# Attention and two feed-forward layers on one core: float32 scores for eight head pairs, read-backs as scheduled loads, and another sequence of value products

## The chip, the core and the metric

The kernel runs on one NeuronCore of a Trainium2 chip. TensorE multiplies matrices, VectorE (DVE), ScalarE (ACT) and GpSimd (POOL) work elementwise, and SyncE (SP) issues the DMAs. Each engine takes its instructions strictly in the order in which the program lists them, so an instruction that waits holds back all that stand behind it on the same engine. The metric is device microseconds of the whole launch, the median of several runs.

## The reference

```
q_n, k_n = rmsnorm(q, g_q), rmsnorm(k, g_k)          # 4 batches x 12 heads, 448 rows of 64
scores = q_n @ k_n.T / 8
attn = exp(scores - max(scores)); attn /= attn.sum() + 1e-9
x = (attn @ v) -> 1792 tokens x 768
x = relu(x @ w_in)**2 @ w_out                        # layer 1, 2048 wide
out = (silu(x @ w_gate) * (x @ w_val)) @ w_out2      # layer 2, 1536 wide
```

Everything is float32. A product of two float32 matrices is mostly made of three faster products: each operand is split into a high part that the fast float32r format holds exactly and a low remainder, and high x high, high x low and low x high are added up (`mm3`).

## The kernel before

Heads are taken in 24 pairs (7 tiles of 128 rows by 448 columns each, since 2 x 448 = 7 x 128; tile 3 holds rows of both heads). For each tile TensorE makes the scores (`sc`, L723 and L729), DVE takes the row maximum (L751) and scales it (L754), ACT takes the exponential into `ring` (L760), TensorE transposes (`pt`, L818 to L828), ACT or DVE copies the result out (`p`, L218), and TensorE multiplies by the values (`o`, L881); DVE divides by the row sums (`ox`, L895).

Scores come in two forms. A pair listed in `FULL_S` is multiplied in float32 straight from the loaded tile `kq_p`: one instruction of the program for a tile, which the trace shows as two (L723). For any other pair `prep_k` and `prep_q` first split k and q of each head into high and low parts (`kst`, `qst`: casts on ACT, subtractions on POOL or DVE, L639 to L660), and TensorE makes two float32r products for each head in a tile, 16 for a pair (L729). Before, `FULL_S` holds pair 0 alone.

While pairs are worked, TensorE fills gaps with products of layer 1 for two finished batches (`h_a`, `ya`: "filler"), and DVE decodes weights, which come as 64-bit words. A first few dozen transposes of the identity (`warm`, L1002) run at the very start.

After attention, layer 1 runs in seven sweeps over a batch (x tokens of 448) and a range of the hidden width. Each needs its activations read back from DRAM and split (`xr` and `x`, `load_x`), and sweeps that finish an earlier partial sum read it back too (`yp`, `Partial`), add to it (L1190) and store it. The raw tiles come from a pool of seven, `io`. Layer 2 takes batches in two pairs and forms each 2x2 block product with seven products instead of eight (`PRODUCTS`, a Strassen-like scheme): operands of weights are formed ahead and spilled to DRAM (`md`), then read into `ring` as `mr` and split; operands of activations are `xq` and `xm` (`x_quarter`, `x_rest`). For each of six steps `fp` there is a gate stage (`hp_g`), a value stage (`hp_v`) and an output stage (`yo`), which wants `s_v` of the value stage, the second half of the hidden rows first (b = 1: products 3 and 7).

The order of everything is made by a planner inside the program. Work items are generator threads with a rank; each yields costs in ns per engine that may do it, a bare number (wait so long), or a condition. `simulate` steps a clock and hands each free engine the ready item of lowest rank. What it emits is a fixed order for each engine; semaphores do the waiting on the chip. A DMA issued through `dma(...)` costs the planner time and continues the thread when the planner thinks it has landed. In `Partial.load` before, the read of a partial sum is issued directly and is known to the planner as no work at all: the tile counts as there at once. In `load_x` before, one tile is read, cast and subtracted before the next is asked for.

## Time and profile before

| | us |
|---|---|
| median of 3 runs | 1338.75 (1335.79 to 1339.97) |
| the profiled execution | 1345.3 |
| its span, first to last instruction | 1343.5 |
| TensorE busy | 1273.7 (95%) |
| DVE busy | 1029.4 (77%) |
| ACT busy | 674.3 (50%) |
| POOL busy | 221.3 (16%) |

In the rows below, "busy" is the time in which at least one instruction of an engine runs; PEclk is the granted share of TensorE's clock, 1.00 for 2.4 GHz and 0.50 for 1.2 GHz. In a row of the timeline, x6 means six like instructions in a row, and the bracket gives the engine's idle time before the first and what ended it. Consecutive matmuls overlap, so their rate is read from start to start.

### The profile page before, as it was taken

How to read it: one execution, taken by the hardware profiler on the slowest of the kernel's cores; microseconds unless marked ns; L12 is line 12 of the kernel's file. 1: busy time of each engine (PE TensorE's matmuls, PEld its weight loads, DVE VectorE, ACT ScalarE, POOL GpSimd, SP SyncE). 2: the span in 40 equal slices, each digit the busy share in tenths (PEclk: the TensorE clock that was granted, in tenths of full speed). 3: DMA queues.
4: the chain of work that ended last, by engine and by line, in shares of the span. 5: the costliest groups of instructions: out<-in, count | busy, mean ns of one | idle time of the engine just before them, and what ended most of it. 6: DMA issues, size and time to landing. Idle time of an engine off the chain costs nothing.

```text
span 1343.5 us, 19657 instructions
## 1 busy us (share of the span) xinstructions
PE 1273.7 (95%) x6306; PEld 1077.3 (80%) x6306; DVE 1029.4 (77%) x2262; ACT 674.3 (50%) x1528; POOL 221.3 (16%) x207
## 2 busy tenths in 40 slices
PE   8787899998999999999999998899999999999998
PEld 6544576666777999999998897799989889999997
DVE  7999997865641788978877897989885687666573
ACT  5788897876854455443332333543443355333331
POOL 3444444543331000000000101010110130000000
PEclk8789999999999999999999899899999989999999
DMA  5676666676422355468687795475443452322222
GB/s 199 202 227 209 199 214 196 204 220 182 154 78 72 104 157 163 139 204 255 198 264 237 234 327 183 148 224 161 148 127 89 141 169 85 106 83 83 82 65 82
DMA packets 125129, 222.13 MB, mean 165 GB/s; under 512 B 17177, under 2 KB 98658, under 8 KB 125026
## 3 DMA queue, kind: packets, MB, share of 16 engines
q1 hardware_dynamic: 125026, 220.89, 52.5%
q8 instruction: 49, 0.80, 0.2%
q14 instruction: 54, 0.44, 0.1%
HBM read 176.03 MB, written 44.80 MB: 164 GB/s over the span
## 4 chain that ended last, share of the span: by engine, by line
PE 69%; DVE 16%; DMA 7%; issue 3%; ACT 2%; SPq 1%; POOL 1%; DVEq 0%; ACTq 0%; POOLq 0%
PE y L341 19%; PE h L341 12%; PE hp_v L341 10%; PE hp_g L341 7%; PE yo L341 6%; PE sc L729 3%; PE o L881 3%; PE h_a L341 2%; DMA zb<-zd 2%; PE ya L341 2%; DVE mr L1339 2%; DVE sc L751 2%; PE pt L828 2%; DVE f_g L1446 1%; DMA rkb<-rkd 1%
## 5 line engine op out<-in xcount | busy, mean ns | idle before, releaser
L341 PE MATMUL y<-s,hi_out 128*128 128x448 f32 x624 | 180.1, 370 | 3.1 <-DVE yp L1190 3.1
L341 PE MATMUL h<-x,hi_in 128*128 128x448 f32 x588 | 167.8, 366 | 1.6 <-DVE r L378 1.6
L751 DVE TENSOR_REDUCE sc<-sc 128x1 f32<-128x448 f32 x168 | 101.8, 625 | 51.8 <-PE sc L729 47.8
L760 ACT ACTIVATE ring<-sc,m,rms 128x448 f32<-128x448 f32 x168 | 121.8, 726 | 34.8 <-DVE m L754 25.0
L341 PEld LDWEIGHTS y<-s,hi_out 128*128 128x128 f32 x624 | 118.6, 190 | 13.6 <-ACT wa_g L272 3.4
L729 PE MATMUL sc<-kst,qst 128*128 128x448 f32 x368 | 110.6, 407 | 15.3 <-ACT ring L760 12.4
L218 ACT CAST mr<-mr 128x384 fp32r<-128x384 f32 x216 | 103.7, 512 | 39.1 <-DMA mr<-md_v_s 10.8
L341 PEld LDWEIGHTS h<-x,hi_in 128*128 128x128 f32 x588 | 110.3, 188 | 11.3 <-DVE r L378 2.0
L1339 DVE TENSOR_TENSOR mr<-mr 128x384 fp32r<-128x384 f32 x194 | 107.9, 577 | 14.8 <-ACT mr L218 14.8
L341 PE MATMUL y<-s,lo_out 128*128 128x448 f32 x312 | 115.0, 369 | 0.0
L341 PE MATMUL hp_g<-xm_t,mr 128*128 128x448 f32 x432 | 98.4, 377 | 10.5 <-DVE xm_t L1364 4.6
L341 PE MATMUL h<-x,lo_in 128*128 128x448 f32 x294 | 107.3, 365 | 0.0
L1446 DVE TENSOR_TENSOR f_v<-f_v,hp_v 128x448 f32<-128x448 f32 x60 | 37.0, 617 | 87.1 <-PE hp_v L341 87.1
L341 PE MATMUL yo<-s_v,mr 128*128 128x448 f32 x432 | 96.1, 378 | 6.2 <-ACT s_v L218 3.8
L218 ACT COPY p<-pt 128x448 f32<-128x448 f32 x166 | 86.2, 530 | 27.6 <-PE pt L828 20.7
L341 PEld LDWEIGHTS hp_g<-xm_t,mr 128*128 128x128 f32 x432 | 82.6, 193 | 20.1 <-DVE xm_t L1364 5.0
L341 PEld LDWEIGHTS yo<-s_v,mr 128*128 128x128 f32 x432 | 82.1, 193 | 18.9 <-DVE f_g L1446 4.7
L341 PE MATMUL hp_v<-xm_t,mr 128*128 128x448 f32 x432 | 94.0, 366 | 0.0
L341 PE MATMUL y<-s_v,mr 128*128 128x448 f32 x432 | 89.9, 366 | 0.0
L729 PEld LDWEIGHTS sc<-kst,qst 128*128 128x128 f32 x368 | 64.4, 199 | 29.2 <-ACT ring L760 16.0
L341 PEld LDWEIGHTS hp_v<-xm_t,mr 128*128 128x128 f32 x432 | 81.2, 188 | 6.8
L341 PEld LDWEIGHTS y<-s_v,mr 128*128 128x128 f32 x432 | 81.1, 188 | 6.8
(174 smaller groups left out, 2621.8 us busy)
## 6 DMA issues: line engine op xcount, KB each, us to landing
kq<-in_kq_t_dram SPq DMA_DIRECT2D x46, 448.0 KB
raw_in<-in_w_in_dram SPq DMA_DIRECT2D x32, 384.0 KB
raw_out<-in_w_out_dram SPq DMA_DIRECT2D x32, 384.0 KB
vz<-in_v_z_dram SPq DMA_DIRECT2D x23, 448.0 KB
rkb<-rkd SPq DMA_DIRECT2D x46, 224.0 KB
raw_o<-in_w_out_dram SPq DMA_DIRECT2D x24, 384.0 KB
raw_g<-in_w_gate_dram SPq DMA_DIRECT2D x24, 384.0 KB
raw_v<-in_w_val_dram SPq DMA_DIRECT2D x24, 384.0 KB
```

Source lines behind the costliest of these rows:

```text
L218: e.copy(out, src)
L341: return {"P": 203}, lambda e: e.matmul(ps, lhsT=w, rhs=x, start=first, stop=last), 0
L729: e.matmul(sc, lhsT=qs[h][:, c, rows], rhs=ks[h], start=(p + c == 0), stop=(p + 1 == len(parts) and c == 1),)
L751: yield {"V": 531}, lambda e: e.tensor_reduce(out=top, in_=sc, axis=AX.X, op=ALU.max, negate=True)
L760: yield {"A": 704}, lambda e: e.activation(out=probs(n, 0, S), in_=sc, func=ACTF.Exp, bias=m, scale=rq, accum_out=sums[g][0][:, i:i + 1])
L828: e.transpose(ps[:, bass.ts(t, 128)], probs((first if j < 3 else second) + t, k, 128), ident)
L881: e.matmul(o[half], lhsT=vz[:, j, half], rhs=ps[j][0], start=(i < 2), stop=(i >= 6))
L1339: yield {"W": 469, "G": 956}, lambda e: e.tensor_tensor(out=lo, in0=as_f32(lo), in1=as_f32(hi), op=ALU.subtract)
L1446: return {"V": 535}, lambda e: e.tensor_tensor(out=out, in0=b, in1=ps, op=how)
```

## The change

`FULL_S` grows from pair 0 to pairs 0 to 7: seven more pairs have their scores made in float32, without `prep_q` and the split of `prep_k`; DVE scales k once for a pair. `warm` goes on: until 90 us of the planner's clock it adds two transposes wherever the planner sees TensorE idle for over 300 ns. It holds a PSUM bank meanwhile that the filler needs. `load_x` starts a thread for each tile, so that several reads are under way, and leaves 3000 ns after the planned landing before it lists the cast. `Partial` reads its tiles through `dma(...)` in threads of their own, with 1500 ns after it. The product with operands (12, 21), which was third of seven, comes last in value stages, and the weights are read in that sequence. `RAW_SLOTS` goes from 7 to 8, which leaves 16 - 5 - 8 = 3 slots instead of 4 for `mr` at the start of layer 2; `x_fetch` leaves three `io` tiles instead of two to others.

```diff
-RAW_SLOTS = 7
+RAW_SLOTS = 8
+X_MARGIN = 3000
+IO_KEPT = 3
-WARM = [1500, 5500, 20000]
-FULL_S = [0]
+WARM = [1500, 5500, 20000, 90000]
+IDLE = 300
+FULL_S = list(range(8))
...
+        while clock[0] < WARM[3]:
+            yield 400
+            if clock[0] - free_at["P"] > IDLE:
+                for _ in range(2):
+                    yield {"P": 110}, lambda e: e.transpose(ps[:, :128], ident, ident), 0
         h_free.append(where)
...
-        def part(j, where):
+        def part(j, where, t):
             raw = tile_at(where, [128, S], F32, f"xr_{n}_{j}")
             yield from dma(lambda e: e.dma_start(out=raw, in_=src[j]), 128 * S * 4)
-            t = tiles(j)
+            yield X_MARGIN
             yield {"A": 467, "W": 300}, lambda e: copy(e, t[:, 0, :], raw)
...
         for j in range(KD):
             yield lambda: io_free
-            yield from part(j, io_free.pop(0))
+            spawn(part(j, io_free.pop(0), tiles(j)), k)
...
         def load(self):
-            while io_free and len(self.tiles) < KD:
-                j = len(self.tiles)
-                self.at[j] = io_free.pop(0)
-                self.tiles[j] = tile_at(self.at[j], [128, S], F32, f"yp_{self.n}_{j}")
-                nc.sync.dma_start(out=self.tiles[j], in_=self.src[j])
+            while io_free and self.next < KD:
+                spawn(self.one(self.next, io_free.pop(0)), self.k)
+                self.next += 1
+
+        def one(self, j, where):
+            t = tile_at(where, [128, S], F32, f"yp_{self.n}_{j}")
+            yield from dma(lambda e: e.dma_start(out=t, in_=self.src[j]), 128 * S * 4)
+            yield MAT_MARGIN
+            self.at[j], self.tiles[j] = where, t
...
+    ORDERS = {"g": PRODUCTS, "v": PRODUCTS[:2] + PRODUCTS[3:] + [PRODUCTS[2]]}
...
-            keys = [(w, fp, m) for _, m, _ in PRODUCTS]
...
+                keys = [(w, fp, m) for _, m, _ in ORDERS[w]]
...
-        keep = [0, 2] if p == 0 else [0, FLATS_KEPT]
+        keep = [0, IO_KEPT] if p == 0 else [0, FLATS_KEPT]
...
-        for i, m, x in PRODUCTS:
+        for i, m, x in ORDERS[w]:
```

On TensorE, the scores of pair 1 (`kst2`, `kst3` are the split k of its two heads, `kq_p1` its loaded tile) stand before as

```order
L729 MATMUL sc7_664<-kst2_636,qst0_247 128x448 x2
L729 MATMUL sc8_670<-kst2_636,qst0_247 128x448 x2
L729 MATMUL sc9_676<-kst2_636,qst0_247 128x448 x2
L729 MATMUL sc10_681<-kst2_636,qst0_247 128x448 x2
L729 MATMUL sc10_681<-kst3_639,qst1_248 128x448 x2
L729 MATMUL sc11_709<-kst3_639,qst1_248 128x448 x2
L729 MATMUL sc12_720<-kst3_639,qst1_248 128x448 x2
```

and now as

```order
L726 MATMUL sc7_621<-kq_p1_293 128x448
L726 MATMUL sc8_648<-kq_p1_293 128x448
L726 MATMUL sc9_656<-kq_p1_293 128x448
L726 MATMUL sc10_667<-kq_p1_293 128x448
L1010 MATMUL warm_264<-ident_205 128x128 x4
L726 MATMUL sc11_685<-kq_p1_293 128x448
L726 MATMUL sc12_693<-kq_p1_293 128x448
```

Sixteen float32r products of a pair become seven in float32, with four transposes of the identity among these. Up to the first score of pair 8, 31 products of the filler stand on TensorE before, and 15 now.

On DVE, where layer 1 ends and layer 2 begins (`yp_1_6` are the partial sums of the last sweep, `xm0` operands of the first batch pair, `f_0_g0_6` the first sum that frees a PSUM bank), there stands before

```order
L1190 TENSOR_TENSOR yp_1_6_2_9277<-y_1_6_2_8948,yp_1_6_2_9277 128x448
L1190 TENSOR_TENSOR yp_1_6_3_9286<-y_1_6_3_8958,yp_1_6_3_9286 128x448
L1364 TENSOR_TENSOR xm0_t2_1_9269<-xq0_12_1_8810,xm0_t2_1_9269 128x448
L1364 TENSOR_TENSOR xm0_t2_2_9270<-xq0_12_2_8933,xm0_t2_2_9270 128x448
L1383 TENSOR_TENSOR xq0_11_1_8809<-xq0_12_1_8810,xq0_11_1_8809 128x448
L1383 TENSOR_TENSOR xq0_11_2_8923<-xq0_12_2_8933,xq0_11_2_8923 128x448
L1383 TENSOR_TENSOR xq0_21_1_8914<-xq0_12_1_8810,xq0_21_1_8914 128x448
L1190 TENSOR_TENSOR yp_1_6_4_9327<-y_1_6_4_8966,yp_1_6_4_9327 128x448
L1446 TENSOR_TENSOR f_0_g0_6_9320<-f_0_g0_1_9299,hp_0_g0_6_9295 128x448
```

and now

```order
L1378 TENSOR_TENSOR xm0_t2_2_9045<-xq0_12_2_8729,xm0_t2_2_9045 128x448
L1378 TENSOR_TENSOR xm0_t3_1_9046<-xq0_11_1_8599,xm0_t3_1_9046 128x448
L1397 TENSOR_TENSOR xq0_11_2_8719<-xq0_12_2_8729,xq0_11_2_8719 128x448
L1378 TENSOR_TENSOR xm0_22_0_9047<-xq0_22_0_8597,xm0_22_0_9047 128x448
L1397 TENSOR_TENSOR xq0_21_2_8744<-xq0_12_2_8729,xq0_21_2_8744 128x448
L1378 TENSOR_TENSOR xm0_t3_2_9083<-xq0_11_2_8719,xm0_t3_2_9083 128x448
L1378 TENSOR_TENSOR xm0_22_1_9048<-xq0_22_1_8601,xm0_22_1_9048 128x448
L1378 TENSOR_TENSOR xm0_22_2_9094<-xq0_22_2_8737,xm0_22_2_9094 128x448
L1378 TENSOR_TENSOR xm0_t4_0_9049<-xq0_21_0_8598,xm0_t4_0_9049 128x448
L1202 TENSOR_TENSOR yp_1_6_3_9062<-y_1_6_3_8733,yp_1_6_3_9062 128x448
L1202 TENSOR_TENSOR yp_1_6_4_9069<-y_1_6_4_8741,yp_1_6_4_9069 128x448
L1460 TENSOR_TENSOR f_0_g0_6_9101<-f_0_g0_1_9076,hp_0_g0_6_9073 128x448
```

The operands of t2 no longer stand behind the additions of `yp` 3 that wait for a read; nine operations on operands come ahead of `yp` 3 and 4, and `f_0_g0_6` still stands behind both.

On TensorE, the end of the last value stage of the first batch pair and the start of its output stage, before:

```order
L341 MATMUL hp_0_v5_3_11525<-xm0_22_2_9378,mr102_11216 128x448 x3
L341 MATMUL hp_0_v5_4_11545<-xm0_t4_0_9271,mr103_11237 128x448 x3
L341 MATMUL hp_0_v5_4_11545<-xm0_t4_1_9333,mr103_11237 128x448 x3
L341 MATMUL hp_0_v5_4_11545<-xm0_t4_2_9379,mr103_11237 128x448 x3
L341 MATMUL yo0_5_0_11565<-s2_0_v5_3_11577,mr104_11254 128x448 x3
```

and now:

```order
L344 MATMUL hp_0_v5_4_11362<-xm0_t4_2_9095,mr102_11055 128x448 x3
L344 MATMUL hp_0_v5_2_11386<-xm0_21_0_8691,mr103_11075 128x448 x3
L344 MATMUL hp_0_v5_2_11386<-xm0_21_1_8967,mr103_11075 128x448 x3
L344 MATMUL hp_0_v5_2_11386<-xm0_21_2_8971,mr103_11075 128x448 x3
L344 MATMUL yo0_5_0_11401<-s2_0_v5_3_11409,mr104_11093 128x448 x3
```

Eighteen matmuls instead of nine now stand between product 3 and the first matmul that wants its result.

## Rows read from the trace of the kernel before

**Rows 1.** By stage: us, busy us of each engine, granted clock, DMA share

```profile
39.60:152.80 113.20, 89.04 (x441) 55.71 (x439) 107.07 (x265) 93.39 (x233) 47.89 (x41) 0.92 0.70 218
152.80:440.00 287.20, 273.63 (x1487) 200.17 (x1487) 187.83 (x479) 203.75 (x523) 111.44 (x98) 0.98 0.53 166
440.00:735.00 295.00, 295.00 (x1451) 271.88 (x1450) 250.50 (x558) 121.29 (x242) 3.12 (x3) 1.00 0.61 192
735.00:752.00 17.00, 12.32 (x46) 10.52 (x45) 16.46 (x34) 6.24 (x13) 3.40 (x3) 0.80 0.78 256
...
824.00:856.00 32.00, 21.30 (x79) 17.35 (x78) 21.23 (x41) 14.37 (x29) 5.25 (x5) 0.79 0.53 170
...
1071.00:1082.00 11.00, 7.00 (x21) 5.51 (x20) 9.09 (x14) 7.05 (x15) 5.43 (x5) 0.69 0.49 159
```

**Rows 2.** TensorE's timeline: float32 scores of pair 0, then split scores

```profile
15.20 1.70 PE L723 MATMUL sc<-kq_p 128*128 128x448 f32 x2
16.69 5.37 PE L1002 MATMUL warm<-ident 128*128 128x128 f32 x32
...
22.46 1.29 PE L723 MATMUL sc<-kq_p 64*128 64x448 f32 x3
...
23.59 0.91 PE L723 MATMUL sc<-kq_p 64*128 64x448 f32 x2
...
106.57 1.46 PE L729 MATMUL sc<-kst,qst 128*128 128x448 f32 x6
107.87 0.27 PE L826 MATMUL pt<-ident,ring 128*128 128x128 f32 x1
```

**Rows 3.** Groups from 39.6 to 152.8 us, DVE and POOL: count, busy, mean ns

```profile
L643 DVE TENSOR_TENSOR kq<-kq,rkb 128x448 f32<-128x448 f32 x9 | 6.6, 728 | 0.7 <-DMA rkb<-rkd 0.7
L640 DVE SCALAR_TENSOR_TENSOR kq<-kq,gqk,rkb 128x448 f32<-128x448 f32 x4 | 2.7, 679 | 0.0
...
L283 DVE SCALAR_TENSOR_TENSOR wt_in<-wa_in,wt_in 128x384 int32<-128x384 int32 x8 | 5.3, 667 | 0.0
...
L660 POOL TENSOR_TENSOR qst<-kq,qst 128x448 fp32r<-128x448 f32 x14 | 17.3, 1236 | 31.6 <-ACT qst L218 24.7 <-DMA vz<-in_v_z_dram 2.7 <-DVE rst L442 2.6
L648 POOL TENSOR_TENSOR kst<-kq,kst 64x448 fp32r<-64x448 f32 x12 | 15.1, 1259 | 17.3 <-ACT kst L218 12.3 <-ACT nat L465 4.5
```

**Rows 4.** DVE from 440 to 735 us, where POOL is idle: the same decoding step

```profile
L283 DVE SCALAR_TENSOR_TENSOR wt_in<-wa_in,wt_in 128x384 int32<-128x384 int32 x18 | 9.9, 551 | 0.0
```

**Rows 5.** The granted clock around the transposes of the identity, columns as in rows 1

```profile
13.30:20.20 6.90, 6.90 (x23) 4.65 (x22) 6.04 (x20) 1.79 (x4) 2.96 (x3) 0.51 0.41 111
20.20:30.40 10.20, 7.48 (x42) 4.72 (x40) 8.62 (x32) 8.35 (x23) 2.93 (x3) 1.00 0.44 134
...
78.20:85.00 6.80, 6.80 (x22) 3.18 (x22) 6.70 (x19) 6.20 (x18) 4.45 (x4) 0.50 0.88 281
```

**Rows 6.** Timeline around 735 us, SP, ACT and DVE

```profile
728.17 0.46 SPq L1100 DMA_DIRECT2D xr<-x1d  x1
...
734.70 0.57 ACT L218 CAST x<-xr 128x448 fp32r<-128x448 f32 x1 [10.55 <-DMA xr<-x1d]
...
735.30 0.63 DVE L1103 TENSOR_TENSOR x<-xr,x 128x448 fp32r<-128x448 f32 x1 [6.18 <-ACT x L218]
```

**Rows 7.** Timeline from 826 to 847 us, DVE and TensorE

```profile
830.87 0.62 DVE L1190 TENSOR_TENSOR yp<-y,yp 128x448 f32<-128x448 f32 x1 [2.51 <-DMA yp<-y1d]
837.37 0.62 DVE L1190 TENSOR_TENSOR yp<-y,yp 128x448 f32<-128x448 f32 x1 [3.20 <-DMA yp<-y1d]
...
832.08 1.87 PE L341 MATMUL hp_g<-xm_t,mr 128*128 128x448 f32 x5 [4.60 <-DVE xm_t L1364]
846.65 2.98 PE L341 MATMUL hp_g<-xm_t,mr 128*128 128x448 f32 x7 [3.04 <-DVE mr L1339]
```

**Rows 8.** TensorE at the end of the first batch pair

```profile
1069.64 2.02 PE L341 MATMUL hp_v<-xm_t,mr 128*128 128x448 f32 x9
1074.78 0.66 PE L341 MATMUL yo<-s_v,mr 128*128 128x448 f32 x1 [3.13 <-ACT s_v L218]
```

More of the change, by code (lines that the diff above doesn't have):

```diff
@@ L1094, in x_tiles, with load_x @@
         return tile_of
-    def load_x(src, n, tiles, done):
-        def part(j, where):
+    def load_x(src, n, tiles, done, k):
+        def part(j, where, t):
             raw = tile_at(where, [128, S], F32, f"xr_{n}_{j}")
             yield from dma(lambda e: e.dma_start(out=raw, in_=src[j]), 128 * S * 4)
-            t = tiles(j)
+            yield X_MARGIN
             yield {"A": 467, "W": 300}, lambda e: copy(e, t[:, 0, :], raw)
@@ L1134, in products @@
                     src = (x1_d if sweeps[i + 1][0] == 1 else x2_d)[sweeps[i + 1][1]]
-                    spawn(load_x(src, n, x_tiles(n, i % 2 == 0, nxt), done), k)
+                    spawn(load_x(src, n, x_tiles(n, i % 2 == 0, nxt), done, k), k)
                 if f == fs[1] and i + 1 == len(sweeps):
@@ L1151, in products @@
                     yield from behind.pop(0)
-                sums = Partial(partial, n) if partial and f == fs[-1] else None
+                sums = Partial(partial, n, k) if partial and f == fs[-1] else None
                 behind.append(out_of(name, n, layer, f, f == fs[0], f == fs[-1], f in last_use, ys, sums, dst, k))
@@ L1171, in attention_two_ffn_kernel, with __init__ @@
     class Partial:
-        def __init__(self, src, n):
-            self.src, self.n, self.tiles, self.at = src, n, {}, {}
+        def __init__(self, src, n, k):
+            self.src, self.n, self.k, self.next, self.tiles, self.at = src, n, k, 0, {}, {}
             self.load()
         def load(self):
-            while io_free and len(self.tiles) < KD:
-                j = len(self.tiles)
-                self.at[j] = io_free.pop(0)
-                self.tiles[j] = tile_at(self.at[j], [128, S], F32, f"yp_{self.n}_{j}")
-                nc.sync.dma_start(out=self.tiles[j], in_=self.src[j])
+            while io_free and self.next < KD:
[6 more added lines that the diff above has]
+            self.at[j], self.tiles[j] = where, t
     def written(ps, sums, j, n, dst):
@@ L1324, in ring_feed @@
         for k, (p, w, fp) in enumerate(stages()):
-            keys = [(w, fp, m) for _, m, _ in PRODUCTS]
             if w == "o2":
                 keys = [(w, 2 * fp + f, c) for f in range(2) for c in range(2)]
+            else:
+                keys = [(w, fp, m) for _, m, _ in ORDERS[w]]
             for key in keys:
```

## The prediction

> **What bounds the kernel now.** The page comes first: TensorE is busy for 95% of the span, DVE for 77%. An average over stages hides where time can be had, so the table by stage comes next [rows 1]. Three kinds of stretch are to be seen in it. From 39.6 to 152.8 us (the scores of pairs 1 to 7) TensorE is busy 89.0 of 113.2 us and DVE 107.1, so DVE is nearly full, TensorE idles 24.2 us, and the granted clock is 0.92. From 152.8 to 440 TensorE idles 13.6 of 287.2 us, and from 440 to 735 not at all: there only less TensorE work would help. Three short stretches stand out: 735 to 752 (12.3 of 17.0 busy, clock 0.80), 824 to 856 (21.3 of 32.0, 0.79) and 1071 to 1082 (7.0 of 11.0, 0.69). Together they hold 4.7 + 10.7 + 4.0 = 19.4 us of idle. Last come the timelines of these, where the bracket names the wait.
>
> **Float32 scores for pairs 1 to 7.** At full clock three instructions of a float32 score start at 22.46 and the fourth at 23.59, so 0.377 us each and 0.754 for a tile of two [rows 2]. Six split products start at 106.57 and the next row at 107.87, so 0.217 each [rows 2]. A pair is now 7 x 0.754 = 5.28 us instead of 16 x 0.217 = 3.47; over seven pairs TensorE gains 12.7 us of work. New transposes stand at 26 places of the order; at a sixth of a microsecond (5.37 us for 32, rows 2, at half clock) they are at most 4 us, and I take 2, since they stand where TensorE was meant to idle.
>
> What goes is preparation. On POOL the two subtractions are 17.3 + 15.1 = 32.4 of its 47.9 us [rows 1, 3]. On DVE the scalings of k are 6.6 + 2.7 = 9.3 us [rows 3]; seven float32 pairs put one back each, 7 x 0.68 = 4.8. DVE gains more than that, because its own work is slow while POOL runs: the same decoding step takes 667 ns here [rows 3] and 551 where POOL is idle [rows 4], 17% of its time. DVE work of this kind is about 60 of its 107 us (the rest are the reductions and what reads PSUM), so some 10 us are such waiting, and two thirds of POOL's time goes: 7 us. DVE comes to 107.1 - 9.3 + 4.8 - 7 = 96.
>
> TensorE's 89.0 us contain work at half clock: 0.92 granted is 18 of 113 us at 1.2 GHz, and at a busy share of 0.79 that cost 7. With 12.7 and 2 more, and 16 filler products fewer before pair 8 (31 before, 15 now, 16 x 0.21 = 3.3), TensorE has 100 us with that loss and 93 without. So DVE and TensorE both want about 95, and a chain through scores, maximum, exponential and transposes will not pack either fully. I take 102 for the stretch, a gain of 11; the 3.3 us of filler come back later, where TensorE is full [rows 1]. **Term: -8.** Bounds: no wait left at all, 95, is -18 + 3 = -15; nothing hidden, every idle microsecond and the low clock kept, is 12.7 + 2 = +15. The row nearest is DVE's 107 of 113, and it says that DVE was what the stretch waited for, so I stay on the side of a gain. From 152.8 to 440 the work is as before and I put 0.
>
> **The clock in idle spells.** From 16.69 to 21.98 nothing but transposes of the identity ran on TensorE [rows 2]; the granted clock was 0.51 up to 20.2 us and 1.00 after it [rows 5], so here transposes alone were followed by the rise to 2.4 GHz. Against this change speaks the Trainium skill (TensorE: Matmul & The Clock Gate, Part 4: PE-mode transpose): it says that full clock does not engage for transposes, since they do not count as busy in the same way. The trace does not bear that out. By the rule the new transposes would leave the low clock as it is, and TensorE would want 100 us in this stretch and not 93.
>
> **Activations read back, around 735 us.** The read of `xr` is issued at 728.17, and ACT, with the cast already at the head of its queue, stands idle 10.55 us until 734.70; DVE idles 6.18 us behind it [rows 6]. Behind these stand the squares of `h` that free a PSUM bank, so TensorE idles 4.7 us in the stretch, and clock 0.80 of 17 us is another 3.4 lost. After the change the planner lists the cast 3 us later than its planned landing, with other ACT work ahead of it. **Term: -7**, bounds 0 and -8.1; late next would be the additions of `yp`, which stand on DVE just behind.
>
> **Sums read back, 824 to 856.** The planner thought `yp` there at once, so DVE stands 2.51 and 3.20 us at additions whose reads are still on the way [rows 7], and behind them stand the operands of t2 (TensorE 4.60 us), sums that free banks, and the split of `mr` (3.04) [rows 7]. Idle is 10.7 us, and clock 0.79 of 32 costs 6.7 more: 17.4 in all. Now the operands come first, and with three `io` tiles instead of two the six sums need fewer rounds of store and read. But `mr` starts with three slots instead of four: the fourth weight is issued on SP behind two reads of sums, which wait for stores, then cast behind three casts of operands; and `f_0_g0_6` still stands behind two sums, with nine operations of 0.54 us or so ahead of them. I estimate 3 us of wait at the fourth product and 1 or 2 at the sixth, and part of the low clock. **Term: -9**, bounds -17 (all gone) and +3 (the new wait for `mr` beside the old ones).
>
> **Value products in another sequence.** At 1069.64 the last nine products of the value stage start, and `yo` starts at 1074.78 after 3.13 us of idle [rows 8]; a second wait makes it 4.0, and clock 0.69 of 11 us adds 3.4. Nine more products, 9 x 0.21 = 1.9 us, now stand between product 3 and its reader. On DVE the addition for product 2 stands ahead of the last step of `s_v` though, so about half of the idle stays. **Term: -3.5**, bounds 0 and -7.4. In other value stages a gate stage lies between, and the sequence costs nothing; u is held four products longer, and what hides that is that two of eleven flat tiles are still free.
>
> **The sum:** -8 - 7 - 9 - 3.5 = -27.5. The profiled execution took 1345.3, so it would be 1317.8; that execution was 6.5 above the median of the runs, and from 1338.75 the sum gives 1311.
>
> **Rivals.**
>
> *Slower: the float32 scores run at half clock.* The tile at 15.20 took 1.49 us to the next start at 16.69 [rows 2], at clock 0.51 [rows 5], twice the 0.754. If TensorE keeps its idle in this stretch and a share s of the 49 tiles runs so, the stretch is 15 + 36 s longer, against 19.5 gained later; from s = 0.15 on the kernel is slower, and at one half it is 15 + 18 - 19.5 = +13.5, 1352. For it: 18 of 113 us were at half clock before, and the filler, which padded such gaps, moves back. Against: each float32 tile keeps TensorE occupied for 0.75 us where there were 0.43, and at 78.2 to 85.0 the low clock met a TensorE without a gap [rows 5], so the low spells are rather what follows earlier idling, which shrinks.
>
> *The early stretch stays a chain of waits.* DVE is relieved but each pair still waits for exponential, transpose and copy; idle and clock stay, float32 is simply added: +15 - 19.5 = -4.5, 1334. For it: float32 scores leave the chain with as many steps as it had. Against: DVE at 107 of 113.
>
> *Transposes do not hold the clock.* The early term is -1 instead of -8: -20.5, 1318. The page named above says so; rows 5 speak against it.
>
> *Three slots for weights spoil the start of layer 2.* The third term is 0: -18.5, 1320. For it: the place of the fourth `mr` behind the sums. Against: the two DVE waits of rows 7 are for sums, and fewer rounds of these remain.
>
> **Chances.** Forecast 0.50, early chain 0.17, three slots 0.13, transposes 0.12, half-clock scores 0.08. A change of 0.3% (4 us) is about what a measurement of this kernel can tell from none. The forecast and the two rivals near 1320 are faster; of the early chain half is faster, the rest the same or a little slower; the half-clock case is slower. That makes 0.84, 0.06 and 0.10. The forecast's own range is 1300 to 1323. All best ends together, -15 - 8 - 17 - 7 = -47, give 1292, and the early chain with a little loss on top 1336; the range 1292 to 1336 leaves out the half-clock case and little else.
>
> **What would show it.** In the changed profile: pair 8's first score at about 142 us instead of 152.8 (the first term), with DVE no longer above 0.9 of the stretch; clock above 0.95 there, if the transposes help; no ACT idle of over 3 us for `xr`, and no TensorE idle near the fifth sweep's end; at the start of layer 2 under 6 us of idle, its first wait for `mr` and not for an operand; about 2 us before `yo` at the end of the first batch pair. The forecast is wrong in its main part if pair 8 starts no earlier than before, or if the idle of the three short stretches is still above 15 us.

## The result, and the profile after

The changed kernel takes 1326.48 us (median of 14 runs, 1320.24 to 1334.92); the kernel before took 1338.66 beside it (14 runs). The ratio is 0.9909, interval 0.9891 to 0.9926: 12.2 us faster. The forecast was 1311, that is 27.5 us faster; the sign was right, the size not, though the time lies in the range. The profiled execution took 1327.7 us (span 1325.9). The one before took 1345.3, which was 6.6 above its median, so the two profiles differ by 17.6 us and the medians by 12.2; below, it is said which of the two a number comes from.

Columns as in [rows 1], of the changed kernel: the same work, that is pairs 1 to 7, the stretch around the read of `xr`, the start of layer 2, the end of the first batch pair.

```profile
38.30:148.70 110.40, 105.17 (x431) 49.62 (x429) 95.33 (x273) 79.58 (x203) 19.31 (x19) 0.92 0.58 180
...
714.40:731.40 17.00, 17.00 (x85) 15.61 (x84) 15.25 (x33) 5.16 (x10) 0.00 (x0) 1.00 0.94 322
810.10:842.10 32.00, 27.27 (x123) 23.77 (x123) 31.42 (x57) 16.07 (x32) 8.71 (x7) 0.95 0.67 207
1050.50:1061.50 11.00, 6.00 (x21) 4.55 (x21) 10.82 (x15) 7.07 (x16) 7.05 (x6) 0.81 0.51 158
```

Against [rows 1]: TensorE's idle in the early stretch fell from 24.2 to 5.2 us and DVE's load from 107.1 to 95.3, but the stretch is only 2.8 us shorter, and the clock is 0.92 as before. The stretch at `xr` has no idle left. At the start of layer 2 TensorE is busy 27.3 of 32 us (21.3 before). The last row is no better than before: 6.0 of 11 us busy.

Two groups that answer to [rows 3, 4]: the split scores' scalings and subtractions are all but gone, and the decoding step takes 551 ns here too, where it took 667 beside POOL.

```profile
L286 DVE SCALAR_TENSOR_TENSOR wt_in<-wa_in,wt_in 128x384 int32<-128x384 int32 x8 | 4.4, 551 | 0.0
...
L643 DVE SCALAR_TENSOR_TENSOR kq<-kq,gqk,rkb 128x448 f32<-128x448 f32 x1 | 0.7, 673 | 0.0
```

ACT at the cast of `xr` (10.55 us of idle in [rows 6]) now idles a quarter of that, and nothing waits behind it:

```profile
722.45 0.57 ACT L221 CAST x<-xr 128x448 fp32r<-128x448 f32 x1 [2.54 <-DMA xr<-x1d]
```

DVE and TensorE at the start of layer 2, answering to [rows 7]: the additions of `yp` wait for no read, and the operands come first. The waits left are 3.20 us at the fourth gate product, for a sum `f_g` that stands on DVE behind operands and two `yp`, and 1.42 us before the first value product.

```profile
815.82 1.41 DVE L1378 TENSOR_TENSOR xm_t<-xq,xm_t 128x448 fp32r<-128x448 f32 x1
817.15 1.14 DVE L1202 TENSOR_TENSOR yp<-y,yp 128x448 f32<-128x448 f32 x2
818.22 0.60 DVE L1460 TENSOR_TENSOR f_g<-f_g,hp_g 128x448 f32<-128x448 f32 x1
...
818.97 5.23 PE L344 MATMUL hp_g<-xm_t,mr 128*128 128x448 f32 x18 [3.20 <-DVE f_g L1460]
829.34 2.06 PE L344 MATMUL hp_v<-xm,mr 128*128 128x448 f32 x9 [1.42 <-ACT sg_g L1510]
```

TensorE at the end of the first batch pair, answering to [rows 8]: the wait did not shrink, it came apart into 0.80, 1.12 and 3.08 us, the last for DVE.

```profile
1052.12 2.09 PE L344 MATMUL hp_v<-xm,mr 128*128 128x448 f32 x9 [0.80 <-DVE f_v L1460]
1055.33 0.48 PE L344 MATMUL yo<-s_v,mr 128*128 128x448 f32 x1 [1.12 <-ACT s_v L221]
1058.89 7.35 PE L344 MATMUL yo<-s_v,mr 128*128 128x448 f32 x23 [3.08 <-DVE s_v L1523]
```

By stretches of the same work, in the two profiles (start to start of the matmuls named, us):

| stretch | before | after |
|---|---|---|
| first scores of pairs 1 to 8 | 113.2 | 110.4 |
| first score of pair 8 to first score of the last pair | 230.1 | 219.4 |
| from there to the last products `o`, with the filler that is left | 37.1 | 45.2 |
| fifth to sixth sweep of layer 1 (`xr`) | 52.1 | 44.2 |
| first gate stage of layer 2 | 29.0 | 19.2 |
| first value product to first `yo` of the last step | 221.1 | 226.0 |

In these two profiles the read-backs won what was forecast (7.9 and 9.8 us), the early part won less, and the first batch pair, where 3.5 us were to be won, lost 4.9. The execution before was a slow one in two of these stretches. From pair 8 to the last pair, three experiments with its early order (e2, e3, e12) took 222.4 to 225.8 us and not 230.1. From the last `o` to layer 2, which the read of `xr` lies in, it took 404.7 us and six experiments with the old read-backs 399.8 to 403.3; with the new ones it is 396.8 to 397.0. So the usual gain there is 3 to 6.5 us and not 7.9.

### The profile page after: what moved, and what is told of

Its sections match the earlier page's. It is cut to its first block, busy times and chain, and to the rows that moved or that the text cites. A ratio compares the mean times of both kernels' runs of the same rounds, so it can differ in the third digit from the quotient of the medians.

```text
span 1325.9 us, 19575 instructions
## 1 busy us (share of the span) xinstructions
PE 1285.5 (97%) x6309; PEld 1064.5 (80%) x6309; DVE 1021.1 (77%) x2245; ACT 654.9 (49%) x1490; POOL 207.2 (16%) x190
## 4 chain that ended last, share of the span: by engine, by line
PE 79%; DVE 11%; DMA 5%; issue 2%; ACT 2%; SPq 0%; DVEq 0%; ACTq 0%
PE y L344 20%; PE h L344 14%; PE hp_v L344 8%; PE hp_g L344 7%; PE yo L344 6%; PE o L884 5%; PE sc L732 3%; PE ya L344 3%; PE h_a L344 3%; PE pt L831 3%; PE sc L726 3%; DVE f_g L1517 2%; DVE mr L1353 2%; DMA zb<-zd 1%; DMA nat<-in_k_n_dram 1%
## 5 line engine op out<-in xcount | busy, mean ns | idle before, releaser
L763 ACT ACTIVATE ring<-sc,m,rms 128x448 f32<-128x448 f32 x168 | 121.6, 725 | 31.7 <-DVE m L757 17.6
L1353 DVE TENSOR_TENSOR mr<-mr 128x384 fp32r<-128x384 f32 x179 | 99.0, 575 | 12.4 <-ACT mr L221 12.1
L344 PE MATMUL h<-x,lo_in 128*128 128x448 f32 x294 | 107.1, 364 | 0.0
L1353 POOL TENSOR_TENSOR mr<-mr 128x384 fp32r<-128x384 f32 x37 | 51.6, 1404 | 322.4 <-DVE f_v L1460 186.0
L379 ACT ACTIVATE r<-h 128x448 f32<-128x448 f32 x49 | 26.6, 542 | 124.1 <-PE h L344 124.1
```

Of the source, the lines that this page charges most:

```text
L344: return {"P": 203}, lambda e: e.matmul(ps, lhsT=w, rhs=x, start=first, stop=last), 0
L379: yield {"A": 424}, lambda e: e.activation(out=r, in_=ps, func=ACTF.Relu)
L763: yield {"A": 704}, lambda e: e.activation(out=probs(n, 0, S), in_=sc, func=ACTF.Exp, bias=m, scale=rq, accum_out=sums[g][0][:, i:i + 1])
L1353: yield {"W": 469, "G": 956}, lambda e: e.tensor_tensor(out=lo, in0=as_f32(lo), in1=as_f32(hi), op=ALU.subtract)
```

## The experiments

Ratios are to the kernel before on the same chip, with 95% intervals; "us" is (ratio - 1) x 1338.7. The kernel before had medians from 1334.8 to 1341.0 in the five sets of runs, so ratios are to be compared, not times.

| run | what it is | ratio | interval | us |
|---|---|---|---|---|
| changed | all of it | 0.9909 | 0.9891 to 0.9926 | -12.2 |
| e1 | changed, old sequence | 0.9869 | 0.9847 to 0.9890 | -17.5 |
| e2 | before, new sequence | 1.0009 | 0.9994 to 1.0024 | +1.2 |
| e3 | before, read-backs | 0.9902 | 0.9878 to 0.9926 | -13.1 |
| e4 | before, scores and idle transposes | 0.9967 | 0.9945 to 0.9989 | -4.4 |
| e5 | before, scores | 1.0001 | 0.9979 to 1.0022 | +0.1 |
| e6 | before, idle transposes | 1.0022 | 1.0001 to 1.0043 | +2.9 |
| e7 | before, scores and read-backs | 0.9900 | 0.9876 to 0.9924 | -13.4 |
| e8 | changed, weights' subtractions on DVE | 0.9844 | 0.9814 to 0.9874 | -20.9 |
| e9 | e8 with the old sequence | 0.9833 | 0.9805 to 0.9861 | -22.4 |
| e10 | e4 without the transposes, bank held | 0.9986 | 0.9963 to 1.0008 | -1.9 |
| e11 | changed, weights' subtractions on POOL | 1.0478 | 1.0451 to 1.0505 | +64.0 |
| e12 | before, weights' subtractions on DVE | 0.9960 | 0.9938 to 0.9982 | -5.4 |
| e13 | e9, products in idle spells | 0.9856 | 0.9831 to 0.9880 | -19.3 |
| e14 | e13, products at the start too | 0.9864 | 0.9833 to 0.9894 | -18.2 |
| e15 | e14 with half as many products | 0.9919 | 0.9889 to 0.9949 | -10.8 |

### Which part did what: e1 to e4

**e1** is the changed kernel with one line put back:

```diff
-    ORDERS = {"g": PRODUCTS, "v": PRODUCTS[:2] + PRODUCTS[3:] + [PRODUCTS[2]]}
+    ORDERS = {"g": PRODUCTS, "v": PRODUCTS}
```

> The changed kernel with the old sequence of value products (12, 21 third again); all else as changed. The changed kernel lost 5 us against before from the first value stage to the first output stage of the last step of the first batch pair (221.1 us before, 226.0 after), and 2 us more behind it. Theory: the new sequence puts the addition for product 2 behind three gate products on DVE, next to the end of the stage, and the bank that it frees is wanted by the next stage; then the stretch returns to about 221 us, the two waits before yo come back to about 4 us, and the time is 1321 (1319 to 1324). Rival: the shorter layer 1 leaves more weight decoding for layer 2 (20 half tiles instead of 14 are begun there on DVE), whatever the sequence; then the stretch stays near 226 and the time near 1326, or 1329 if the sequence gains its 3.5 us.

1319.46 us, and the stretch of the first batch pair takes 222.4 us instead of 226.0: the new sequence costs 5 us in company. The rival falls: it had the stretch stay near 226.

**e2** is the kernel before with this part alone:

```diff
-        for i, m, x in PRODUCTS:
+        for i, m, x in ORDERS[w]:
```

> The kernel before with the new sequence of value products alone. Theory (the sequence costs): the same 5 us in the first batch pair, 1341 to 1345. Rival (decoding left over costs): nothing in the first batch pair, and the wait before yo at the end of the first pair falls from 4.0 us to about 2, 1335 to 1338. The prediction on record had -3.5, 1335.

1339.18 us, between the two: alone the sequence costs nothing that the times can tell. Nor can the profiles: the stretch takes 223.3 us, and 220.8 to 223.9 in five with the old sequence and the old read-backs (before, e4, e5, e6, e10).

**e3** is the kernel before with the threads of `load_x` and `Partial`, and the old `RAW_SLOTS` and `IO_KEPT`.

```diff
-            yield from part(j, io_free.pop(0))
+            spawn(part(j, io_free.pop(0), tiles(j)), k)
...
+        def one(self, j, where):
```

> The kernel before with the new read-backs alone (load_x in threads with 3000 ns, Partial through dma with 1500 ns); sequence, float32 scores, idle transposes, 7 raw slots and 2 io tiles as before. The change gained 7.9 us from the fifth sweep's to the sixth sweep's start and 9.8 us in the first gate stage, in its profile. Theory: both gains come from this part, 16 to 18 us in the profile; timed 12 to 17 us, 1322 to 1327, since a part of them was the low clock, which the runs of before have in differing amounts. Rival: the second gain is the slots' (three io tiles for sums instead of two), then only about 8 us, 1331.

1323.37 us, and the first gate stage takes 16.9 us (29.0 before): the read-backs bring their two gains without the slots.

**e4** is the kernel before with the early part alone.

```diff
-WARM = [1500, 5500, 20000]
-FULL_S = [0]
+WARM = [1500, 5500, 20000, 90000]
+FULL_S = list(range(8))
```

> The kernel before with float32 scores for pairs 0 to 7 and the transposes in idle spells alone. Theory: the early term as the change's profile has it, -6.6 us at the first main sweep's start, so 1330 to 1334. Rival: the early stretch gains no time over many runs, because the profile of before had more low clock than its other runs (its time is 6.6 us above their median); then 1336 to 1341.

1334.06 us. The parts add up: 0.9902 x 0.9967 is 0.9869, just e1, so the slots bring nothing that can be told; and the sequence in company takes 5.4 us back.

### What the sequence and POOL cost: e8, e9, e11, e12

The rows of DVE in the first batch pair (first value product to first `yo` of the last step) seem to point to one group. Before and changed kernel:

```profile
L1446 DVE TENSOR_TENSOR f_v<-f_v,hp_v 128x448 f32<-128x448 f32 x30 | 18.5, 616 | 27.7 <-PE hp_v L341 27.7
L1503 DVE TENSOR_TENSOR f_g<-f_v,f_g 128x448 f32<-128x448 f32 x23 | 14.3, 647 | 0.0
```

```profile
L1517 DVE TENSOR_TENSOR f_g<-f_v,f_g 128x448 f32<-128x448 f32 x23 | 21.6, 974 | 0.0
L1460 DVE TENSOR_TENSOR f_v<-f_v,hp_v 128x448 f32<-128x448 f32 x29 | 17.7, 613 | 17.5 <-PE hp_v L344 17.4
```

The sum whose two inputs both lie in SBUF went from 647 to 974 ns; the sum that reads one input from PSUM did not change. POOL meanwhile has more weights to split there, since the planner put 37 of the 216 subtractions on it instead of 22 (22 and 13 in this stretch). The sequence is not all of that: with the old one e1 has 25 and e3 30. Nor does their number alone set the sum: e3, with 21 in this stretch, has it at 723 ns. One place in the changed kernel, POOL, DVE and TensorE:

```profile
922.97 3.54 POOL L1353 TENSOR_TENSOR mr<-mr 128x384 fp32r<-128x384 f32 x3 [1.15 <-ACT mr L221]
926.73 1.15 POOL L1353 TENSOR_TENSOR mr<-mr 128x384 fp32r<-128x384 f32 x1 [0.22 <-ACT mr L221]
...
924.47 3.89 DVE L1517 TENSOR_TENSOR f_g<-f_v,f_g 128x448 f32<-128x448 f32 x3
928.28 0.61 DVE L1460 TENSOR_TENSOR f_v<-f_v,hp_v 128x448 f32<-128x448 f32 x1
...
928.94 2.09 PE L344 MATMUL hp_g<-xm_t,mr 128*128 128x448 f32 x9 [1.14 <-DVE f_v L1460]
```

Three sums take 1.3 us each, about the time of one subtraction on POOL; behind them stands the addition of the value product that now comes last, and behind that TensorE's next bank. **e8** takes POOL away:

```diff
-        yield {"W": 469, "G": 956}, lambda e: e.tensor_tensor(out=lo, in0=as_f32(lo), in1=as_f32(hi), op=ALU.subtract)
+        yield {"W": 469}, lambda e: e.tensor_tensor(out=lo, in0=as_f32(lo), in1=as_f32(hi), op=ALU.subtract)
```

> The changed kernel with the subtraction that splits a weight (mr) listed for DVE alone; 37 of them stood on POOL, 22 of these in layer 2's first batch pair. Theory (POOL at work beside DVE lengthens DVE's sums, f_g at 974 ns against 647 before, and that is how the value sequence costs 7 us here): 1320 to 1323, f_g of the first batch pair at 700 ns or less, that stretch from the first value product to the first output product 220 to 223 us instead of 226.0. Rival (DVE is simply too full there: 20 decoding half tiles are left to it instead of 14, and 22 x 0.55 = 12 us of subtractions more do not help): 1326 to 1332, the stretch 226 us or longer, with the same waits for f_g and s_v.

It gained more than the theory said: 20.9 us on the kernel before, 8.7 more than the changed kernel. The stretch takes 223.1 us instead of 226.0. DVE there:

```profile
L1460 DVE TENSOR_TENSOR f_v<-f_v,hp_v 128x448 f32<-128x448 f32 x29 | 17.8, 613 | 12.9 <-PE hp_v L344 10.9 <-ACT mr L221 1.9
L1517 DVE TENSOR_TENSOR f_g<-f_v,f_g 128x448 f32<-128x448 f32 x23 | 14.8, 665 | 0.0
```

The sum is back at 665 ns. The two waits before `yo` in e8's timeline:

```profile
1045.64 0.47 PE L344 MATMUL yo<-s_v,mr 128*128 128x448 f32 x1 [1.25 <-ACT s_v L221]
1047.18 3.23 PE L344 MATMUL yo<-s_v,mr 128*128 128x448 f32 x8 [1.07 <-DVE s_v L1523]
```

They were 1.12 and 3.08. Not all of the 8.7 us is POOL's: of the 12.8 us between the two profiles, 7.4 lie ahead of layer 2, where e8 was at 1.2 GHz less in the same order of work; 2.9 lie in the stretch and 3.0 behind it.

**e9** is e8 with the old sequence too:

```diff
+    ORDERS = {"g": PRODUCTS, "v": PRODUCTS}
...
+        yield {"W": 469}, lambda e: e.tensor_tensor(out=lo, in0=as_f32(lo), in1=as_f32(hi), op=ALU.subtract)
```

> The changed kernel with the old sequence of value products and the weights' subtractions on DVE alone: two steps at once. Times for a kernel before at 1338.7. Theory (what the sequence cost was POOL's company; without POOL the new sequence brings the 1 to 3 us before the output stage that it was made for): 1317 to 1321, that is no faster than the old sequence with POOL (ratio 0.9869) and 0 to 4 us slower than the new sequence without POOL (ratio 0.9844). Rival (the sequence costs 7 us of its own, and keeping weights off POOL is a separate gain): 1306 to 1312, both gains added up.

0.9833, a hair under the theory's range and far from the rival's: the times cannot tell the two sequences apart (0.9844 and 0.9833). The profiles can, and they side with the rival. The stretch, e8 and then e9 (columns as in [rows 1]), and what TensorE waited for up to the first `yo` (us in total, times, longest):

```profile
822.50:1045.60 223.10, 218.68 (x1054) 195.97 (x1052) 190.65 (x378) 93.53 (x197) 10.41 (x8) 1.00 0.52 157
PE yo L344 <- DVE f_g L1460: 1.5, 2, 1.2
PE yo L344 <- ACT s_v L221: 1.2, 1, 1.2
PE hp_v L344 <- DVE f_v L1460: 0.8, 2, 0.4
PE hp_g L344 <- DVE f_v L1460: 0.6, 1, 0.6
PE yo L344 <- DVE acc L1576: 0.2, 1, 0.2
...
829.50:1047.90 218.40, 216.21 (x1055) 196.61 (x1053) 189.34 (x381) 95.39 (x199) 7.86 (x6) 1.00 0.53 161
PE yo L344 <- ACT s_v L221: 1.3, 1, 1.3
PE hp_v L344 <- DVE f_v L1460: 0.7, 1, 0.7
PE hp_g L344 <- DVE f_v L1460: 0.2, 1, 0.2
```

With no weight on POOL the new sequence still costs 4.7 us there, and behind the stretch the two kernels are alike (267.5 and 267.6 us). All profiles but e11's, where the weights are on POOL:

| first batch pair, us | old sequence | new sequence |
|---|---|---|
| old read-backs, with POOL | 221.1 (before), 220.8 to 223.9 (e4, e5, e6, e10) | 223.3 (e2) |
| new read-backs, with POOL | 222.4 (e1), 224.2 and 224.3 (e7 and e3, old slots) | 226.0 (changed) |
| old read-backs, without POOL | 218.7 (e12) | - |
| new read-backs, without POOL | 218.4 (e9), 218.2 to 218.4 (e13 to e15) | 223.1 (e8) |

Where POOL is away, five profiles with the old sequence lie within 0.5 us and the one with the new sequence 4.4 or more above them. With POOL the changed kernel lies 3.6 us above e1, which differs from it in the sequence alone, and a further 2.2 behind the stretch. POOL costs 2.9 us in the stretch with the new sequence (226.0 and 223.1) and 4.0 with the old (222.4 and 218.4). The two profiled executions hide it in their whole time: up to the last `o`, where both have the same order of work, e9 was 8 us behind e8, at 1.2 GHz for 23.9 us between pairs 1 and 8 where e8 was for 6.8. The few timed runs with the same mean granted clock show it too: at 0.984 e9 took 1316.9 and 1317.3 us and e8 1321.0, at 0.987 they took 1314.3 and 1318.4. Of the 4.7 us, 2.1 lie in the five gate stages and 2.2 in the output stages behind them. Waits of TensorE for sums on DVE make 3.1 us in e8 and 0.9 in e9; which row of DVE's new order holds these sums up is not shown.

**e11** is the changed kernel with all 216 on POOL:

```diff
-        yield {"W": 469, "G": 956}, lambda e: e.tensor_tensor(out=lo, in0=as_f32(lo), in1=as_f32(hi), op=ALU.subtract)
+        yield {"G": 956}, lambda e: e.tensor_tensor(out=lo, in0=as_f32(lo), in1=as_f32(hi), op=ALU.subtract)
```

> The changed kernel with all 216 subtractions of the weights on POOL instead of 37 (DVE is relieved of 179, some 98 us of work). Theory (each subtraction on POOL, 1.3 us, slows what DVE does beside it): the f_g sum (L1517) of the first batch pair stays at 900 ns or more, layer 2 is no shorter in spite of the relief, and the whole takes 1327 to 1345. Rival (DVE is simply too full in the first batch pair): the relief shortens that stretch from 226 to 221 us or less, and the whole takes 1314 to 1322.

Both were wrong by far: 1404.06 us. DVE has some 98 us less to do and the kernel is 76 us slower than the changed one (ratios 1.0478 and 0.9909), 0.43 us for each subtraction moved; low clock is part of that (38.9 us at 1.2 GHz in the stretch, none in the changed kernel). DVE, same stretch of e11:

```profile
L1517 DVE TENSOR_TENSOR f_g<-f_v,f_g 128x448 f32<-128x448 f32 x23 | 21.4, 952 | 0.1
L1460 DVE TENSOR_TENSOR f_v<-f_v,hp_v 128x448 f32<-128x448 f32 x29 | 17.8, 616 | 56.2 <-PE hp_v L344 31.5 <-ACT mr L221 24.4
```

So relieving DVE by way of POOL does not help: DVE now stands idle 56 us ahead of the sums of value products, and the sum of two SBUF inputs stays slow. Whether a full DVE is part of what the sequence costs, this run does not show. The Trainium skill (SBUF — State Buffer, section "SBUF: two separate sides") says that DVE and GpSimd contend for one port pair, exclusively and for a whole instruction, when the DVE operation has two SBUF inputs and the GpSimd operation reads SBUF. The traces agree: 974 and 952 ns with two inputs in SBUF, 613 and 616 with one in PSUM.

**e12** puts e8's line into the kernel before:

```diff
+        yield {"W": 469}, lambda e: e.tensor_tensor(out=lo, in0=as_f32(lo), in1=as_f32(hi), op=ALU.subtract)
```

> The kernel before with its 22 subtractions of weights on POOL moved to DVE, and nothing else. Theory (POOL costs only where DVE is the one that is waited for; before, DVE waits 27.7 us for value products in that stretch): no change, ratio 0.998 to 1.001, the first batch pair (first value product to first output product) 220 to 222 us as before (221.1). Rival (POOL costs wherever it works): ratio 0.994 to 0.997, that stretch 217 to 219 us.

The rival was right: 0.9960, and the stretch takes 218.7 us instead of 221.1, the one behind it 265.9 instead of 268.7. POOL cost 5.4 us (2.4 to 8.3) before too. TensorE before `yo`, old sequence, without POOL:

```profile
1064.87 0.47 PE L344 MATMUL yo<-s_v,mr 128*128 128x448 f32 x1 [1.38 <-ACT s_v L221]
1066.94 1.28 PE L344 MATMUL yo<-s_v,mr 128*128 128x448 f32 x5 [1.61 <-DVE s_v L1526]
```

The first wait, 3.13 us in [rows 8], became 1.38 with the products in their old sequence, but the second grew from 0.88 to 1.61: together 4.0 became 3.0. Without POOL the new sequence has 2.3 there (1.25 and 1.07 in e8) and the old one 3.0 (1.35 and 1.61 in e9), so what it was made for is worth some 0.6 us.

### Why the early part won so little: e5, e6, e7, e10

**e5** and **e6** split e4, the scores alone and the idle transposes alone; against the kernel before these are

```diff
-FULL_S = [0]
+FULL_S = list(range(8))
```

```diff
-WARM = [1500, 5500, 20000]
+WARM = [1500, 5500, 20000, 90000]
```

> The kernel before with float32 scores for pairs 0 to 7 and nothing else; no transposes in idle spells. The order now has 35 filler products before pair 8, where scores and transposes together had 15. Theory (the transposes do not hold the clock where other work surrounds them, and cost filler that is then done later where TensorE is full, 20 x 0.21 = 4 us): 1330 to 1334, 0 to 4 us faster than scores with transposes (1334.06), with as much or less time at 1.2 GHz before pair 8. Rival (the transposes do hold the clock, and without them the float32 scores run slower): 1337 to 1342, with more than 27 us at 1.2 GHz between the first scores of pairs 1 and 8.

> The kernel before with transposes of the identity in idle spells until 90 us of the planner's clock (140 instead of 74 in all) and nothing else; scores of pairs 1 to 7 split as before. Theory (they do not hold the clock; 66 transposes stand in gaps and cost 0 to 3 us): 1337 to 1341, with 14 to 28 us at 1.2 GHz between the first scores of pairs 1 and 8, as before (17.1 in the profiled execution before). Rival (they hold the clock): 1330 to 1334, with under 8 us at 1.2 GHz there.

e5 came out at the rival's time (1339.64, ratio 1.0001) without the rival's cause: 9.5 us at 1.2 GHz between the first scores of pairs 1 and 8, where that rival wanted over 27. e6 (1344.56) refutes its rival: 17.1 us at 1.2 GHz, as before, and 22.8 us of idle. Neither half brings anything; together they bring 4.4 us. The profiles show why so little is hard to see: up to the last `o`, three other runs with the old early part (e2, e3, e12) take 412.0 to 415.2 us, and six with the new one (changed, e1, e4, e8, e9, e11) 405.7 to 413.9; the scores without the transposes (e5, e7) take 417.2 and 416.1.

**e7** is e1 without the idle transposes and with the old slots, against the changed kernel:

```diff
-RAW_SLOTS = 8
-IO_KEPT = 3
-WARM = [1500, 5500, 20000, 90000]
+RAW_SLOTS = 7
+IO_KEPT = 2
+WARM = [1500, 5500, 20000, 0]
...
+    ORDERS = {"g": PRODUCTS, "v": PRODUCTS}
```

> Float32 scores for eight pairs and the two read-backs as scheduled loads; the sequence of the value products, the slots (RAW_SLOTS 7, IO_KEPT 2) and the idle spells as before. Theory (the slots and the transposes bring nothing): 1315 to 1320, equal to or a little faster than the changed kernel with the old sequence (1319.46), with a first gate stage of layer 2 of 17 to 19 us. Rival (the slots carry part of the second gain, or the transposes part of the first): 1322 to 1327, with 21 us or more in the first gate stage or more time at 1.2 GHz before pair 8.

0.9900, the rival's time, 4 us behind e1, as e5 behind e4. The first gate stage is 16.9 us, so it is not the slots. They even cost some 2 us in that stage: with the old slots it takes 16.9 us (e3, e7), with the new ones 19.2 (changed) and 19.0 (e1). The first batch pair behind it gives that back (224.3 and 224.2 us in e3 and e7, 222.4 in e1).

**e10** is e4 without the transposes: the bank stays held, and the filler stays away.

```diff
             if clock[0] - free_at["P"] > IDLE:
-                for _ in range(2):
-                    yield {"P": 110}, lambda e: e.transpose(ps[:, :128], ident, ident), 0
+                pass
```

> The kernel before with float32 scores for pairs 0 to 7 and with the PSUM bank of the idle transposes held until 90 us, but without the transposes: 15 filler products before pair 8, as with them, against 35 without the hold. Times for a kernel before at 1338.7. Theory (what the idle transposes brought beside float32 scores, 0.34%, is the filler kept away until TensorE is full anyway; the transposes themselves do nothing): 1332 to 1336, ratio 0.995 to 0.998, from pair 8 to the last scores 217 to 220 us as with the transposes. Rival (the transposes themselves bring it): 1338 to 1342, with more time at 1.2 GHz before pair 8 than the 27 us there with them.

Between both: 0.9986. From pair 8 to the last pair it takes 220.4 us (218.6 in e4, 223.1 in e5), and from the start to the last `o`, by when the filler put off is made up, 410.8 (412.5 and 417.2). That speaks for the filler, but it is one profile of each, and the three intervals overlap. How the 4 us arise stays open.

### The low clock: e13 to e15

Idle went, low clock stayed, and then TensorE's own rate sets the early stretch. The first five have the same 431 instructions of TensorE in it:

| between first scores of pairs 1 and 8 | us | idle | us at 1.2 GHz |
|---|---|---|---|
| e8 | 105.5 | 4.5 | 6.8 |
| e1 | 110.0 | 6.1 | 13.6 |
| changed | 110.4 | 5.2 | 17.0 |
| e9 | 112.0 | 3.6 | 23.9 |
| e4 | 113.7 | 3.6 | 27.3 |
| e14 (products) | 105.7 | 6.2 | 0 |

From e8 to e4 that is 8.2 us longer for 20.5 us more at 1.2 GHz, 0.4 us for each; the three between them lie at 0.4 to 0.7. In e4 the clock fell after 5.57 busy of 7 us and stayed down over 27.3 us without any idle (columns as in [rows 1]):

```profile
35.00:42.00 7.00, 5.57 (x20) 2.44 (x18) 6.84 (x23) 4.90 (x13) 0.00 (x0) 1.00 0.74 223
42.00:69.30 27.30, 27.30 (x68) 12.50 (x69) 17.72 (x50) 13.45 (x36) 5.22 (x5) 0.50 0.38 122
69.30:85.00 15.70, 15.70 (x75) 7.41 (x71) 12.80 (x43) 11.71 (x30) 1.13 (x1) 1.00 0.52 142
```

What ran in those 27.3 us were float32 scores, transposes of `ring`, four transposes of the identity, a few small ones, and from 64.23 on the products `o`. **e13** and **e14** put products of the identity in place of its transposes, first in idle spells, then also at the start:

```diff
-                    yield {"P": 110}, lambda e: e.transpose(ps[:, :128], ident, ident), 0
+                    yield {"P": 110}, lambda e: e.matmul(ps[:, :128], lhsT=ident, rhs=ident, start=True, stop=True), 0
```

> The kernel of the run before with the old sequence and the weights on DVE (ratio 0.9833), with one more edit: the 26 instructions in idle spells are products of the identity with itself instead of its transposes; every engine's order is the same. Theory A (transposes do not hold the clock in company, products do): under 10 us at 1.2 GHz between the first scores of pairs 1 and 8 (17.0, 13.6, 27.3, 6.8 and 23.9 in the five profiles with transposes), ratio 0.978 to 0.981, 1309 to 1313 for a kernel before at 1338.7. Rival (the low clock is not a matter of what fills these gaps, since TensorE is busy 95% there either way): 10 to 27 us at 1.2 GHz, ratio 0.982 to 0.987.

> As the run before it, and the transposes of the identity in the first 20 us are products too. Theory A (products count for the clock, transposes do not): the low clock between about 12 and 20 us goes as well, some 7 us at half clock less, that is ratio 0.975 to 0.980, with the first score of pair 1 at 31 to 34 us instead of 34.6. Rival (the clock rises after either): the low clock at the start stays 6.8 us or longer, the first score of pair 1 at 34 to 38 us, ratio 0.982 to 0.988.

In both the clock came out as theory A has it and the time as the rival has it; e13's 6.8 us at 1.2 GHz are no less than e8 had with transposes. e14 is not at 1.2 GHz at all before 159 us; its early stretch, in one row:

```profile
38.90:144.60 105.70, 99.54 (x443) 48.33 (x442) 95.83 (x276) 78.70 (x204) 19.12 (x19) 1.00 0.63 191
```

But a product of the identity stands in the trace as two instructions, and the first score starts at 14.0 us instead of 9.9. **e15** has half as many:

```diff
-            yield {"P": WARM_T if clock[0] > WARM[1] else 220}, lambda e: e.transpose(ps[:, :128], ident, ident), 0
+            yield {"P": 2 * WARM_T if clock[0] > WARM[1] else 440}, lambda e: e.matmul(ps[:, :128], lhsT=ident, rhs=ident, start=True, stop=True), 0
```

> As the run with products for all transposes of the identity, but half as many of them (33 at the start, 16 in idle spells), since one product stands in the trace as two instructions and takes twice a transpose. Theory A (products keep the clock up, and their doubled length hid it: the first score started at 14.0 us instead of 10.4): first score back at 10 to 11 us, no more than 7 us at 1.2 GHz before pair 8, ratio 0.978 to 0.983, 1309 to 1316 for a kernel before at 1338.7: the best version. Rival (it was the number of products, not their kind, that held the clock): 10 us or more at 1.2 GHz before pair 8, ratio 0.984 to 0.988.

The rival was right: 0.9919, with 34 us at 1.2 GHz before pair 8 (0 in e14, 13.6 in e13, 13.6 to 34 with transposes beside float32 scores). The kind alone does not decide it. (Its order differs a little more than that: 10 filler products stand before pair 8 instead of 15.) The mean granted clock of the timed runs was 0.983 in e9, 0.987 in e13, 0.990 in e14 and 0.981 in e15, while the ratios of e9, e13 and e14 cannot be told apart.

e8 and e9 have the lowest ratios; both beat the kernel before by 1.2% at least and the changed kernel too, whose interval theirs do not touch. From e13 and e14 they cannot be told.

## Why the prediction was right or wrong

**Activations and sums read back (-7 and -9): right.** Together -16 were forecast, and e3 measured -13.1 (interval -16.3 to -9.9). The two profiles show 7.9 (3 to 6.5 by the other executions) and 9.8, each by the mechanism named: no cast and no addition waits for a read with others queued behind it, and the low clock that followed the idle went with it (0.80 to 1.00 in the first, 0.79 to 0.95 in the second). One detail was wrong: the wait of 3.20 us at the fourth product is there, but for `f_g` on DVE behind the operands, not for `mr`. The rival of three slots falls, since its term of 0 came to 9.8; the slots cost some 2 us of that stage, which the next stretch gives back.

**Float32 scores (-8): the relief came as forecast, the time did not.** DVE came to 95.3 us (96 forecast), TensorE's scores to 51.7 us of busy time and, at full clock throughout, to 47.5 in e14, against 35.0 before, where 17.1 us of the stretch were at 1.2 GHz (12.7 more forecast). The step that failed is "TensorE has 100 us with that loss and 93 without", and the clock above 0.95: TensorE was busy 105.2 us at 0.92, and in e14, where no low clock is left, still 99.5. Pair 8's first score came at 148.7 us, not at 142. So 102 for the stretch lies below even the one without any low clock (105.7 in e14). The 17.0 us of low clock cost some 5 (110.4 against 105.5 in e8, with 6.8, and 105.7 in e14). Which part of the sum made 93 too small by 6 is not shown. In time the term is -4.4 (e4).

**The clock in idle spells: wrong.** From [rows 5] I read that transposes alone are followed by the rise to full clock, and so I expected them to hold it. In company they did not: seven profiles with them (changed, e1, e4, e6, e8, e9, e11) had 6.8 to 27.3 us at 1.2 GHz between the first scores of pairs 1 and 8, and seven without (before, e2, e3, e5, e7, e10, e12) 6.8 to 23.9. The rise in [rows 5] was one event, and the float32 scores of pair 0 stood just ahead of those transposes. The Trainium skill (TensorE: Matmul & The Clock Gate, Part 4: PE-mode transpose) says that full clock does not engage for transposes. e14 agrees with that, e15 does not bear out that kind alone decides; the page's rule gave 1318 as a rival, nearer than the forecast, and its early term of -1 against -4.4 measured is about as far off as -8.

**The value sequence (-3.5): wrong in sign.** It cost 5.4 us in time (changed against e1). The step that failed is "in other value stages a gate stage lies between, and the sequence costs nothing": without any weight on POOL the first batch pair still takes 4.7 us more with the new sequence (223.1 in e8, 218.4 in e9), 4.3 of it in the gate and output stages behind the value stages, and in the whole stretch TensorE waits 3.1 us for sums on DVE instead of 0.9. I had covered the flat tiles that hold u and not read DVE's new order in those stages. At the end of the last value stage, where -3.5 was forecast, the two waits before `yo` came to 2.3 us instead of 3.0 without POOL, and to 4.2 instead of 4.0 with it (changed against e1). POOL is a cost of its own, which the kernel before had too (5.4 us, e12); where a product's addition stands behind slowed sums, as at 928.94 us in the changed kernel, TensorE waits for that too. The price of POOL beside DVE stood in my own comparison of 667 and 551 ns; I used it for the early stretch and did not look for it here.

**The sum.** -13.1, -4.4 and +5.4 make -12.1, and -12.2 was measured. Of the 15.3 us missing, 8.9 are the sequence, 3.6 the early part and 2.9 the read-backs. I had counted from a profile 6.6 us above its median. That shows in the read-backs, since around `xr` it was slower than six others with the same reads; in the early stretch it was not (113.2 us, against 113.8 to 115.4 in e2, e3 and e12).

## What to carry to other kernels

Where an engine is chosen by who is free, count what the choice costs the neighbour: a subtraction on POOL looked free, and each cost 0.2 to 0.4 us of the whole (5.4 us for 22 in e12, 76 for 179 in e11). Before an idle share is booked as a gain, work out how long the stretch would take at the clock it has, since work put into the gaps runs at that clock as well. A change of sequence is to be read in the new order of all engines, not of the one whose sequence it is. Where two kernels differ in one stage and their times cannot be told apart, compare that stage in the profiles: a low clock elsewhere hid 4.7 us between e8 and e9.

## What the runs showed of the hardware

In the first batch pair, a DVE sum with both inputs in SBUF takes 629 to 674 ns in the profiles with 0 to 16 subtractions on POOL there, 723 to 743 with 17 to 21 (e2, e3, e7), 974 with 22 in the changed kernel and 952 with 97 in e11; one with an input in PSUM takes 611 to 619 in every run. The granted clock can stay at half for 27.3 us in which TensorE is never idle (e4), and in the same early part be full throughout (e14).
